# Attention plus SwiGLU on one Trainium2 core: group loads on 128 partitions, x by quadrants, and a DMA transpose of the normalised q

## The chip, the cores and the metric

The kernel runs on one core of a Trainium2 chip. Its time is the device time of one execution in microseconds. I quote medians of several executions. "Span" is the time from the first to the last instruction in a profile; it is about 2 us shorter than the timed value of the same execution (348.6 against 350.33 us before the change). A run is called slow when it lies over 1.5% above the fastest run of its kernel. In the views, PE is TensorE, PEld its loading of weights, DVE VectorE, ACT ScalarE, POOL GpSimd and SP the sync engine, and a q behind a name stands for that engine's sequencer, which issues its DMAs. PSUM is the memory that the matmuls of this kernel write to, in eight buffers that I call banks.

The kernel before was timed at 352.37 us when the prediction was made (median of 3 runs, 352.28 to 354.62).

## The reference, cut to what matters

```python
# q, k, v: [batch 8, heads 8, seq 576, head_dim 64], float32
q_s = exp(q - max(q, -1));  q_s = q_s / sum(q_s, -1)      # softmax over head_dim
k_s = exp(k - max(k, 2));   k_s = k_s / sum(k_s, 2)       # softmax over seq
kv  = einsum('bhsd,bhse->bhde', k_s, v)                   # 64 x 64 for each head
attn = einsum('bhsd,bhde->bhse', q_s, kv)
x   = attn.transpose(0, 2, 1, 3).reshape(4608, 512)       # tokens x (head, dim)
out = (silu(x @ w_gate) * (x @ w_val)) @ w_out            # d_ff 1536
```

The three large products are nearly all of the arithmetic. The attention needs q with the head dimension on the partitions (so q is transposed), and it needs x with its 512 features on the partitions, because x is the streamed operand of the gate and value products.

## The kernel before: the parts that matter

The kernel keeps x transposed in `xt` and works through one batch of attention ahead of the products. A batch has two groups of four heads. A group is loaded with heads on the two halves of the 128 partitions, each half by its own DMA:

```python
def load(b, G, what, src, second=None, after=None):
    t_ = ld.tile([128, 2, T * 64], FP32, tag=what, name=what)
    for g in range(2):                      # two DMAs, each to 64 partitions
        ap = bass.AP(tensor=src.tensor, offset=src[b, 4 * G + 2 * g].offset,
                     ap=[[T * 64, 64], [HSTR, 2], [1, T * 64]])
        ...
        d = eng.dma_start(out=t_[64 * g:64 * g + 64], in_=ap)
```

The attention of a group is a "head" (`att_exp` and `att_norm`: two exponentials on ScalarE, a cast of v, then a sum, a reciprocal and a multiplication on VectorE that give `qs`) and three steps:

```python
def att_t(b, G, eng):        # step 1: nine TensorE transposes of qs, copied out of PSUM
    for t0, t1 in BANKS:
        for t in range(t0, t1):
            nc.tensor.transpose(out=tp[...], in_=s["qs"][:, t, :], identity=ident)
        copy(eng, qt[:, :, t0:t1, :], tp[...])
def att_kv(b, G): ...        # step 2: k'v, 18 matmuls of 64 rows; its 129th column is the sum of k'
def att_bd(b, G): ...        #         k'v divided by that sum, into block-diagonal tiles bd
def att_x(b, G):             # step 3: x, full 128x128 matmuls with bd as weights
    for g in range(2):
        nc.tensor.matmul(out=xp[g], lhsT=s["bd"][:, g, :], rhs=qt[:, g, 0:512], ...)
        nc.tensor.matmul(out=tl[:, g, :], lhsT=s["bd"][:, g, :], rhs=qt[:, g, 512:S], ...)
    ...                      # three copies from PSUM to xt
```

`m_unit(c0, n, m)` is eight matmuls, four for gate and four for value, of one 128-wide slice of d_ff; ScalarE then applies silu (`sg`) and VectorE multiplies (`hr`). `o_unit(j)` is twelve matmuls of the output product. The schedule after batch 0 is written by hand:

```python
        ...                                   # batch 0: attention, then 12 m_units of 576 columns
        att_head(1, 0); o_unit(0); att_head(1, 1); load_batch(2); ...   # batch 1
        chunks = [(S, 448)] + [(c, 512) for c in range(1024, n_tok, 512)]
        for ci, (c0, n) in enumerate(chunks):         # chunk ci carries attention of batch ci + 2
            ...
            for m in range(MT):
                if m in (4, 8):
                    if att:
                        G = 0 if m == 4 else 1
                        att_head(b, G)
                        steps = att_steps(b, G)
                        if G == 1 and b + 1 < B:
                            load_batch(b + 1)
                    if ci > 0:
                        o_unit(...); o_unit(...)      # the first chunk has none
                m_unit(c0, n, m)
                if m % 4 > 0 and m > 4 and steps:
                    steps.pop(0)()
```

The first chunk is special. It has no `o_unit` in it, so TensorE has less work there between a head and the step that needs it.

The softmax here doesn't subtract the row's maximum and nothing guards it: scores larger than these inputs give would overflow.

Of the kernel before, what the change touches and what calls it, by code (L numbers as in the profile page):

```python
# [15 lines left out]
def kernel(  # L16
# [7 lines left out]
    moe_w_out: bass.AP,  # L24
    out: bass.AP,
):



# [4 lines left out]
    nc = tc.nc  # L34
# [24 lines left out]
    hr = const.tile([128, MT, RING], BF16, name="hr", tag="hr")  # L59
    ident = const.tile([128, 128], BF16, name="ident", tag="ident")  # L60
    vbs = [const.tile([128, T, 130], BF16, name=f"vb{i}", tag=f"vb{i}") for i in range(2)]
    bds = [const.tile([128, 2, 128], BF16, name=f"bd{i}", tag=f"bd{i}") for i in range(2)]

    dmas = {}
    raw = {}

    def load(b, G, what, src, second=None, after=None):
        t_ = ld.tile([128, 2, T * 64], FP32, tag=what, name=what)
        for g in range(2):
            ap = bass.AP(  # L70
                tensor=src.tensor,
                offset=src[b, 4 * G + 2 * g].offset,
                ap=[[T * 64, 64], [HSTR, 2], [1, T * 64]],
            )
            eng = second if g == 1 and second is not None else nc.sync
            d = eng.dma_start(out=t_[64 * g:64 * g + 64], in_=ap)  # L76
            if after is not None and g == 0:
                tc.add_manual_dep(d.ins, after.ins.name, SYNC, reason="order of loads")
        dmas[what, b, G] = d
        raw[what, b, G] = t_  # L80

    def load_batch(b, after=None):
        for G in range(NG):
            for what, src in (("q", q), ("k", k), ("v", v)):
                load(b, G, what, src, nc.scalar if (b, G, what) == (0, 0, "q") else None, after)
                after = None

    def w_slice(dst, src, c0, n):
# [23 lines left out]
    BANKS = ((0, 5), (5, 9))  # L112

    def att_exp(b, G, v_eng):
        s = st[b, G] = {"bd": bds[G], "vb": vbs[G]}
        for what in ("q", "k"):
            e = at.tile([128, T, 2, 64], BF16, tag="e" + what, name="e" + what)
            nc.scalar.activation(  # L118
                out=e, in_=raw[what, b, G].rearrange("p h (t d) -> p t h d", d=64), func=AF.Exp
            )  # L120
            s["e" + what] = e
        copy(
            v_eng,
            s["vb"][:, :, 0:128].rearrange("p t (h d) -> p t h d", d=64),
            raw["v", b, G].rearrange("p h (t d) -> p t h d", d=64),
        )
# [18 lines left out]
    def att_t(b, G, eng):  # L145
        s = st[b, G]
        qt = at.tile([128, 2, T, 64], BF16, tag="qt", name="qt")
        for t0, t1 in BANKS:
            tp = psp.tile([128, 1024], BF16, tag="ps", name="tp")
            for t in range(t0, t1):  # L150
                j = t - t0
                nc.tensor.transpose(  # L152
                    out=tp[:, j * 128:(j + 1) * 128], in_=s["qs"][:, t, :], identity=ident
                )
            copy(
                eng,
                qt[:, :, t0:t1, :],
                tp[:, 0:(t1 - t0) * 128].rearrange("p (t g c) -> p g t c", g=2, c=64),
            )
        s["qt"] = qt  # L160

    def att_kv(b, G):
        s = st[b, G]
# [9 lines left out]
                    stop=(t == T - 1),  # L173
                )

    def att_bd(b, G):
        s = st[b, G]
        for g in range(2):
            kv = s["kv"][g]
            kvr = at.tile([128, 1], FP32, tag=f"kvr{g}", name="kvr")  # L180
            nc.vector.reciprocal(out=kvr, in_=kv[:, 128:129])
            for h in range(2):
                r = slice(64 * h, 64 * h + 64)
                nc.vector.tensor_scalar_mul(s["bd"][r, g, r], kv[r, r], kvr[r, :])

    def att_x(b, G):
        s = st.pop((b, G))
        qt = s["qt"].rearrange("p g t c -> p g (t c)")
        xp = [f_tile("xp") for _ in range(2)]
        tl = f_tile("x_tail").rearrange("p (g c) -> p g c", g=8)  # L190
        for g in range(2):
            nc.tensor.matmul(  # L192
                out=xp[g], lhsT=s["bd"][:, g, :], rhs=qt[:, g, 0:512], start=True, stop=True
            )
            nc.tensor.matmul(  # L195
                out=tl[:, g, :], lhsT=s["bd"][:, g, :], rhs=qt[:, g, 512:S],
                start=True, stop=True,
            )
        c0 = b * S
        nc.scalar.copy(out=xt[:, 2 * G, c0:c0 + 512], in_=xp[0])  # L200
        nc.vector.tensor_copy(out=xt[:, 2 * G + 1, c0:c0 + 512], in_=xp[1])  # L201
        nc.scalar.copy(out=xt[:, 2 * G:2 * G + 2, c0 + 512:c0 + S], in_=tl[:, 0:2, :])


    def m_unit(c0, n, m):
        ms = slice(m * 128, (m + 1) * 128)
        parts = [(c0, n)] if n <= 512 else [(c0, n // 2), (c0 + n // 2, n // 2)]
        gu = []
        for w, nm in ((wg, "g_ps"), (wv, "u_ps")):
            ps = [f_tile(nm) for _ in parts]  # L210
            for kk in range(KT):
                for p_, (c, w_) in zip(ps, parts):
                    nc.tensor.matmul(  # L213
                        out=p_[:, 0:w_], lhsT=w[:, kk, ms], rhs=xt[:, kk, c:c + w_],
                        start=(kk == 0), stop=(kk == KT - 1),
                    )
            gu.append(ps)
        for g_ps, u_ps, (c, w_) in zip(gu[0], gu[1], parts):
            r = c % RING
            sg = ff.tile([128, 512], BF16, tag="sg", name="sg")  # L220
            nc.scalar.activation(out=sg[:, 0:w_], in_=g_ps[:, 0:w_], func=AF.Silu)  # L221
            nc.vector.tensor_mul(hr[:, m, r:r + w_], sg[:, 0:w_], u_ps[:, 0:w_])  # L222
# [38 lines left out]
    with tc.manual_schedule():  # L261
# [3 lines left out]
        nc.scalar.activation(out=warm, in_=warm, func=AF.Exp)  # L265
        for vb in vbs:
            nc.vector.memset(vb[:, :, 128:129], 1.0)
        for bd in bds:
            nc.vector.memset(bd, 0.0)

        w_dma = []
        for c0, n in ((0, 256), (256, 384), (640, 384), (1024, 512)):
# [11 lines left out]
        att_norm(0, 1, BANKS)  # L284
        att_t(0, 1, nc.scalar)
        att_kv(0, 1)
        att_bd(0, 0)
        att_x(0, 0)
        att_bd(0, 1)
        att_x(0, 1)  # L290

        load_batch(1, w_dma[-3])
# [8 lines left out]
        def att_steps(b, G):  # L301
            def kv_bd():
                att_kv(b, G)
                att_bd(b, G)
            return [lambda: att_t(b, G, nc.vector), kv_bd, lambda: att_x(b, G)]

        att_head(1, 0)
        o_unit(0)
# [14 lines left out]
        for ci, (c0, n) in enumerate(chunks):  # L323
# [1 line left out]
            first_o = 4 * ci  # L325
            att = b < B
            final = ci == len(chunks) - 1
            steps = []
            for m in range(MT):
                if m in (4, 8):  # L330
                    if att:
                        G = 0 if m == 4 else 1
                        att_head(b, G)
                        steps = att_steps(b, G)
                        if G == 1 and b + 1 < B:
                            load_batch(b + 1)
                    if ci > 0:
                        o_unit(first_o + (0 if m == 4 else 2))
                        if not (final and m == 8):
                            o_unit(first_o + (1 if m == 4 else 3))  # L340
                m_unit(c0, n, m)
                if m % 4 > 0 and m > 4 and steps:
                    steps.pop(0)()
        o_unit(first_o + 3)
        last = n_tok // 128 - 4
        for j in range(last, last + 3):
# [32 lines left out]
```

## Time and profile before

| stage of the trace before | us |
|---|---|
| start to the first gate matmul (attention of batch 0) | 25.29 |
| gate and value of batch 0 | 24.77 |
| batch 1: four output units and attention of batch 1 | 17.92 |
| first chunk (448 columns, attention of batch 2) | 27.96 |
| the rest: five chunks with attention (one of them measured: 35.01 us), two without, and the end | 252.61 |

The stages are cut at the first gate matmul, the first output matmul, the first gate matmul of 448 columns and the first of 512 columns.

The page of the kernel before shows, for each engine, busy time and instructions; then the busy tenths of TensorE and its granted clock in 40 slices of 8.7 us; then the shares of the chain that ended last:

```profile
PE 317.0 (91%) x1900; PEld 159.5 (46%) x1900; DVE 188.5 (54%) x354; ACT 152.6 (44%) x217; POOL 27.2 (8%) x31
PE   0269998998699999999999999999999999999994
PEclk9999999899999999999999999999999999999999
PE 80%; DVE 7%; DMA 7%; ACT 3%; issue 1%; SPq 1%; DVEq 0%; ACTq 0%
```

TensorE bounds the kernel after the first 100 us: its slices read 9. Before that they read 0, 2, 6, then 8, 8 and 6 in the middle. Those are the start, batch 1 and the first chunk.

The windows of the kernel before at the start give busy time (and instructions) of each engine, then the granted clock, the DMA share and GB/s:

```profile
core 0: us, PE busy (x) PEld busy (x) DVE busy (x) ACT busy (x) POOL busy (x), PEclk, DMA share, GB/s
4.00:8.00 4.00, 0.00 (x0) 0.00 (x0) 0.70 (x1) 1.16 (x1) 0.00 (x0) 1.00 1.05 221
8.00:12.00 4.00, 1.21 (x9) 0.89 (x10) 3.26 (x6) 1.72 (x2) 0.34 (x1) 1.00 1.04 227
12.00:16.00 4.00, 1.16 (x18) 0.89 (x17) 0.77 (x1) 1.75 (x2) 4.00 (x6) 1.00 1.05 229
```

TensorE and ScalarE are mostly idle, and the DMA share reads full (1.04 to 1.05) at 221 to 229 GB/s. (VectorE is busy for 3.26 us of the second window, and GpSimd fills the third with issuing the loads of the weights.) The start is bound by loads.

In the timeline of the kernel before, the two transposes of the first chunk are the only waits of TensorE over 2 us after batch 0's attention (columns: start, duration, engine, line, what, and in brackets the idle time before it and what ended it):

```profile
80.12 0.68 PE L152 MATMUL tp<-ident,qs 128*128 128x128 bf16 x9 [2.41 <-DVE qs L138]
91.18 0.68 PE L152 MATMUL tp<-ident,qs 128*128 128x128 bf16 x9 [3.10 <-DVE qs L138]
```

The timeline of TensorE in a full chunk of the kernel before shows what the three steps cost. Matmuls overlap (the gate group at 147.40 lasts 1.03 us, and the next starts 0.86 us after it), so the cost of a group is the distance to the next start, not its duration:

```profile
130.89 0.94 PE L213 MATMUL g_ps<-xt,wg 128*128 128x512 bf16 x3
132.01 0.38 PE L213 MATMUL g_ps<-xt,wg 128*128 128x512 bf16 x1 [0.18 <-DVE xt L201]
132.22 1.02 PE L213 MATMUL u_ps<-xt,wv 128*128 128x512 bf16 x4
...
146.90 0.67 PE L152 MATMUL tp<-ident,qs 128*128 128x128 bf16 x9
147.40 1.03 PE L213 MATMUL g_ps<-xt,wg 128*128 128x512 bf16 x4
...
151.59 0.38 PE L192 MATMUL xp<-qt,bd_78 128*128 128x512 bf16 x1
```

Nine transposes take 0.50 us (146.90 to 147.40). From the start of x at 151.59 to the next group at 152.08 it is 0.49 us. k'v takes 0.63 us (149.22 to 149.85, not shown). The first three lines are the first gate group behind the last x of a batch: its fourth matmul waits for a copy to `xt`, and the group takes 1.33 us (130.89 to 132.22) where a group of four takes 0.86 elsewhere (147.40 to 148.26, not shown).

### The profile page before, as it was taken

How to read it: one execution, taken by the hardware profiler on the slowest of the kernel's cores; microseconds unless marked ns; L12 is line 12 of the kernel's file. 1: busy time of each engine (PE TensorE's matmuls, PEld its weight loads, DVE VectorE, ACT ScalarE, POOL GpSimd, SP SyncE). 2: the span in 40 equal slices, each digit the busy share in tenths (PEclk: the TensorE clock that was granted, in tenths of full speed). 3: DMA queues.
4: the chain of work that ended last, by engine and by line, in shares of the span. 5: the costliest groups of instructions: out<-in, count | busy, mean ns of one | idle time of the engine just before them, and what ended most of it. 6: DMA issues, size and time to landing. Idle time of an engine off the chain costs nothing.

```text
span 348.6 us, 5035 instructions
## 1 busy us (share of the span) xinstructions
PE 317.0 (91%) x1900; PEld 159.5 (46%) x1900; DVE 188.5 (54%) x354; ACT 152.6 (44%) x217; POOL 27.2 (8%) x31
## 2 busy tenths in 40 slices
PE   0269998998699999999999999999999999999994
PEld 0237773444344454444444444444445444444443
DVE  2553439647746674667466746674667433333331
ACT  3454353376655734563456345634663311322200
POOL 0620012111100011002100110011000000000000
PEclk9999999899999999999999999999999999999999
DMA  7999998999602990299029902990202021102123
GB/s 168 228 200 206 226 230 198 230 255 224 131 0 47 231 248 5 60 224 241 5 59 222 244 5 55 212 229 34 51 11 61 1 63 29 31 2 60 30 62 91
DMA packets 25577, 42.81 MB, mean 123 GB/s; under 512 B 2896, under 2 KB 8784, under 8 KB 25552
## 3 DMA queue, kind: packets, MB, share of 16 engines
q1 hardware_dynamic: 19440, 37.33, 46.6%
q0 software_dynamic: 5808, 4.72, 8.6%
q10 hardware_dynamic: 304, 0.43, 0.5%
q8 instruction: 15, 0.25, 0.3%
q14 instruction: 10, 0.08, 0.1%
HBM read 37.75 MB, written 9.44 MB: 135 GB/s over the span
## 4 chain that ended last, share of the span: by engine, by line
PE 80%; DVE 7%; DMA 7%; ACT 3%; issue 1%; SPq 1%; DVEq 0%; ACTq 0%
PE u_ps L213 25%; PE g_ps L213 25%; PE o_ps L238 24%; DMA v<-in_v_dram 5%; PE kv L168 2%; PE tp L152 2%; DMA k<-in_k_dram 2%; DVE xt L201 1%; DVE hr L222 1%; PE xp L192 1%; DVE qs L138 1%; DVE rs L132 1%; ACT L118 1%; ACT eq L118 1%; SPq L76 1%
## 5 line engine op out<-in xcount | busy, mean ns | idle before, releaser
L221 ACT ACTIVATE sg<-g_ps 128x512 bf16<-128x512 f32 (+2 forms) x120 | 65.0, 554 | 146.0 <-PE g_ps L213 145.9
L222 DVE TENSOR_TENSOR hr<-sg,u_ps 128x512 bf16<-128x512 bf16 (+2 forms) x120 | 74.8, 633 | 91.2 <-PE u_ps L213 89.5
L213 PE MATMUL g_ps<-xt,wg 128*128 128x512 bf16 (+2 forms) x480 | 114.1, 361 | 1.2 <-DVE xt L201 0.9
L213 PE MATMUL u_ps<-xt,wv 128*128 128x512 bf16 (+2 forms) x480 | 111.3, 359 | 0.0
L238 PE MATMUL o_ps<-wo,hr 128*128 128x512 bf16 x420 | 94.1, 380 | 0.0
L213 PEld LDWEIGHTS <-wv 128*128 128x128 bf16 x480 | 47.1, 98 | 49.0 <-issue 3.1
L213 PEld LDWEIGHTS <-wg 128*128 128x128 bf16 x480 | 45.2, 99 | 43.0 <-issue 2.0
L238 PEld LDWEIGHTS <-hr 128*128 128x128 bf16 x420 | 40.7, 98 | 49.0 <-issue 0.8
L132 DVE TENSOR_REDUCE rs<-eq 128x18 f32<-128x1152 bf16 x16 | 21.6, 1353 | 32.9 <-ACT eq L118 32.9
L243 DVE COPY o_sb<-o_ps 128x512 f32<-128x512 f32 x35 | 23.2, 685 | 22.1 <-PE o_ps L238 22.1
L152 PE MATMUL tp<-ident,qs 128*128 128x128 bf16 x144 | 12.2, 236 | 19.5 <-DVE qs L138 19.4
L138 DVE TENSOR_TENSOR qs<-eq,rr 128x1152 bf16<-128x1152 bf16 (+2 forms) x18 | 21.9, 1224 | 0.5
L108 POOL CAST vb_76<-v 128x1152 bf16<-128x1152 f32 x7 | 9.2, 1310 | 150.3 <-DMA v<-in_v_dram 89.1
L152 PEld LDWEIGHTS <-qs 128*128 128x128 bf16 x144 | 9.9, 105 | 24.0 <-DVE qs L138 21.2
L118 ACT ACTIVATE eq<-q 128x1152 bf16<-128x1152 f32 x16 | 18.6, 1163 | 4.8 <-DMA q<-in_q_dram 4.6
L118 ACT ACTIVATE ek<-k 128x1152 bf16<-128x1152 f32 x16 | 18.4, 1150 | 4.4 <-DMA k<-in_k_dram 4.4
L221 ACT ACT_TABLE_LOAD x14 | 18.0, 1283 | 0.2
L200 ACT CAST xt<-xp 128x512 bf16<-128x512 f32 x16 | 9.4, 586 | 17.6 <-PE xp L192 9.4
L118 ACT ACT_TABLE_LOAD x13 | 16.7, 1283 | 0.2
L168 PEld LDWEIGHTS <-ek 64*128 64x128 bf16 x288 | 9.7, 102 | 8.5 <-ACT sg L221 5.0
L201 DVE CAST xt<-xp 128x512 bf16<-128x512 f32 x16 | 10.9, 684 | 3.4 <-PE x_tail L195 3.4
L108 POOL CAST vb_77<-v 128x1152 bf16<-128x1152 f32 x7 | 9.0, 1289 | 44.9 <-DMA v<-in_v_dram 24.9
(38 smaller groups left out, 102.0 us busy)
## 6 DMA issues: line engine op xcount, KB each, us to landing
k<-in_k_dram SPq DMA_DIRECT2D x32, 288.0 KB, 8.8
v<-in_v_dram SPq DMA_DIRECT2D x32, 288.0 KB, 9.7
out_dram<-o_sb SPq DMA_DIRECT2D x70, 128.0 KB, 2.4
q<-in_q_dram SPq DMA_DIRECT2D x31, 288.0 KB, 7.7
wo<-in_moe_w_out_dram POOLq DMA_DIRECT2D x3, 512.0 KB, 18.7
wg<-in_moe_w_gate_dram POOLq DMA_DIRECT2D x2, 384.0 KB, 11.0
wv<-in_moe_w_val_dram POOLq DMA_DIRECT2D x2, 384.0 KB, 12.2
wg<-in_moe_w_gate_dram POOLq DMA_DIRECT2D x1, 512.0 KB, 16.8
```

The lines of the kernel that those rows point to most:

```text
L108: eng.tensor_copy(out=out, in_=in_)
L118: nc.scalar.activation(out=e, in_=raw[what, b, G].rearrange("p h (t d) -> p t h d", d=64), func=AF.Exp)
L132: nc.vector.reduce_sum(out=rs, in_=eq2, axis=mybir.AxisListType.X)
L138: nc.vector.tensor_mul(qs[:, t0:t1, :].rearrange("p t (h d) -> p (t h) d", d=64), eq2[:, 2 * t0:2 * t1, :], rr[:, 2 * t0:2 * t1].to_broadc ...
L152: nc.tensor.transpose(out=tp[:, j * 128:(j + 1) * 128], in_=s["qs"][:, t, :], identity=ident)
L168: nc.tensor.matmul(out=kv[g][:, 0:129], lhsT=s["ek"][r, t, :, :].rearrange("p h d -> p (h d)"), rhs=s["vb"][r, t, 0:129], start=(t == 0), ...
L201: nc.vector.tensor_copy(out=xt[:, 2 * G + 1, c0:c0 + 512], in_=xp[1])
L213: nc.tensor.matmul(out=p_[:, 0:w_], lhsT=w[:, kk, ms], rhs=xt[:, kk, c:c + w_], start=(kk == 0), stop=(kk == KT - 1),)
L221: nc.scalar.activation(out=sg[:, 0:w_], in_=g_ps[:, 0:w_], func=AF.Silu)
L222: nc.vector.tensor_mul(hr[:, m, r:r + w_], sg[:, 0:w_], u_ps[:, 0:w_])
L238: nc.tensor.matmul(out=o_ps, lhsT=hr[:, m, r0:r0 + 128], rhs=wo[:, m, :], start=(m == 0), stop=(m == MT - 1),)
L243: nc.vector.tensor_copy(out=o_sb, in_=o_ps)
```

## The change

The intent has three parts.

1. A group tensor is loaded by one DMA to all 128 partitions instead of two to 64 each. The two partition halves now hold heads 4G+g and 4G+2+g instead of 4G+2g and 4G+2g+1.
2. x is computed by 64x64 quadrants, so that a head can be read from one half of the partitions and written to the other. The block-diagonal tiles go. In batch 0, the scaling of k'v is shared by VectorE and ScalarE.
3. From batch 2 on, a DMA transposes `qs` from SBUF to SBUF, and TensorE no longer does it. The heads and steps are moved one unit earlier (in the first chunk, the heads three).

```diff
-        for g in range(2):
-            ap = bass.AP(..., offset=src[b, 4 * G + 2 * g].offset,
-                         ap=[[T * 64, 64], [HSTR, 2], [1, T * 64]])
-            d = eng.dma_start(out=t_[64 * g:64 * g + 64], in_=ap)
+        ap = bass.AP(..., offset=src[b, 4 * G].offset,
+                     ap=[[T * 64, 128], [2 * HSTR, 2], [1, T * 64]])
+        d = nc.sync.dma_start(out=t_, in_=ap)
 ...
+    def att_t_dma(b, G):
+        qt = at.tile([128, T, 2, 64], BF16, tag="qtd", name="qtd")
+        nc.sync.dma_start_transpose(out=qt.rearrange("p t g c -> p t (g c)"),
+                                    in_=s["qs"].rearrange("p t c -> p (t c)"))
 ...
-                nc.vector.tensor_scalar_mul(s["bd"][r, g, r], kv[r, r], kvr[r, :])
+                if split and g == 1:
+                    nc.scalar.mul(kn[r, g, :], kv[r, r], kvr[r, :])
+                else:
+                    nc.vector.tensor_scalar_mul(kn[r, g, :], kv[r, r], kvr[r, :])
 ...
+        for t0, t1 in BANKS:
+            for g in range(2):
+                for h in range(2):
+                    r = slice(64 * h, 64 * h + 64)
+                    nc.tensor.matmul(out=xp[h][64 * g:64 * g + 64, 0:n]...,
+                                     lhsT=s["kn"][r, g, :], rhs=s["qt"][g][r, t0:t1, :], ...)
 ...
-                if m in (4, 8):                       # heads of the two groups
+            heads = {1: 0, 5: 1} if ci == 0 else {3: 0, 7: 1}
+                if att and m in heads:
+                    att_head(b, G)
+                    att_t_dma(b, G)
+                    for i, f in enumerate(att_steps(b, G)):
+                        steps[4 + 4 * G + i] = f      # nothing, kv and bd, x
```

Two smaller edits are not shown. The first q load, of which ScalarE's queue had issued one half, now goes through the sync queue whole. And an `m_unit` of batch 0 is cut into 320 and 256 columns instead of 288 and 288.

More of the change, by code (lines that the diff above doesn't have):

```diff
@@ L61, with load @@
     vbs = [const.tile([128, T, 130], BF16, name=f"vb{i}", tag=f"vb{i}") for i in range(2)]
-    bds = [const.tile([128, 2, 128], BF16, name=f"bd{i}", tag=f"bd{i}") for i in range(2)]
     dmas = {}
     raw = {}
-    def load(b, G, what, src, second=None, after=None):
+    def load(b, G, what, src, after):
         t_ = ld.tile([128, 2, T * 64], FP32, tag=what, name=what)
-        for g in range(2):
-            ap = bass.AP(
-                tensor=src.tensor,
-                offset=src[b, 4 * G + 2 * g].offset,
-                ap=[[T * 64, 64], [HSTR, 2], [1, T * 64]],
-            )
-            eng = second if g == 1 and second is not None else nc.sync
-            d = eng.dma_start(out=t_[64 * g:64 * g + 64], in_=ap)
-            if after is not None and g == 0:
-                tc.add_manual_dep(d.ins, after.ins.name, SYNC, reason="order of loads")
+        ap = bass.AP(
+            tensor=src.tensor,
+            offset=src[b, 4 * G].offset,
+            ap=[[T * 64, 128], [2 * HSTR, 2], [1, T * 64]],
+        )
+        d = nc.sync.dma_start(out=t_, in_=ap)
+        if after is not None:
+            tc.add_manual_dep(d.ins, after.ins.name, SYNC, reason="order of loads")
         dmas[what, b, G] = d
@@ L84, in load_batch @@
             for what, src in (("q", q), ("k", k), ("v", v)):
-                load(b, G, what, src, nc.scalar if (b, G, what) == (0, 0, "q") else None, after)
+                load(b, G, what, src, after)
                 after = None
@@ L114, in att_exp @@
     def att_exp(b, G, v_eng):
-        s = st[b, G] = {"bd": bds[G], "vb": vbs[G]}
+        s = st[b, G] = {"vb": vbs[G]}
         for what in ("q", "k"):
@@ L159, in att_t @@
             )
-        s["qt"] = qt
+        s["qt"] = [qt[:, g, :, :] for g in range(2)]
+    def att_t_dma(b, G):
+        s = st[b, G]
+        qt = at.tile([128, T, 2, 64], BF16, tag="qtd", name="qtd")
+        nc.sync.dma_start_transpose(
+            out=qt.rearrange("p t g c -> p t (g c)"),
+            in_=s["qs"].rearrange("p t c -> p (t c)"),
+        )
+        s["qt"] = [qt[:, :, g, :] for g in range(2)]
     def att_kv(b, G):
@@ L174, in att_kv, with att_bd @@
                 )
-    def att_bd(b, G):
+    def att_bd(b, G, split):
         s = st[b, G]
+        kn = s["kn"] = at.tile([128, 2, 64], BF16, tag="kn", name="kn")
         for g in range(2):
@@ L183, in att_bd @@
                 r = slice(64 * h, 64 * h + 64)
-                nc.vector.tensor_scalar_mul(s["bd"][r, g, r], kv[r, r], kvr[r, :])
+                if split and g == 1:
+                    nc.scalar.mul(kn[r, g, :], kv[r, r], kvr[r, :])
+                else:
+                    nc.vector.tensor_scalar_mul(kn[r, g, :], kv[r, r], kvr[r, :])
     def att_x(b, G):
         s = st.pop((b, G))
-        qt = s["qt"].rearrange("p g t c -> p g (t c)")
-        xp = [f_tile("xp") for _ in range(2)]
-        tl = f_tile("x_tail").rearrange("p (g c) -> p g c", g=8)
-        for g in range(2):
-            nc.tensor.matmul(
-                out=xp[g], lhsT=s["bd"][:, g, :], rhs=qt[:, g, 0:512], start=True, stop=True
-            )
-            nc.tensor.matmul(
-                out=tl[:, g, :], lhsT=s["bd"][:, g, :], rhs=qt[:, g, 512:S],
-                start=True, stop=True,
-            )
-        c0 = b * S
-        nc.scalar.copy(out=xt[:, 2 * G, c0:c0 + 512], in_=xp[0])
-        nc.vector.tensor_copy(out=xt[:, 2 * G + 1, c0:c0 + 512], in_=xp[1])
-        nc.scalar.copy(out=xt[:, 2 * G:2 * G + 2, c0 + 512:c0 + S], in_=tl[:, 0:2, :])
+        for t0, t1 in BANKS:
+            n = 64 * (t1 - t0)
+            xp = [f_tile("xp") for _ in range(2)]
+            for g in range(2):
+                for h in range(2):
+                    r = slice(64 * h, 64 * h + 64)
+                    nc.tensor.matmul(
+                        out=xp[h][64 * g:64 * g + 64, 0:n].rearrange("p (t c) -> p t c", c=64),
+                        lhsT=s["kn"][r, g, :],
+                        rhs=s["qt"][g][r, t0:t1, :],
+                        start=True, stop=True,
+                    )
+            c0 = b * S + 64 * t0
+            nc.scalar.copy(out=xt[:, 2 * G, c0:c0 + n], in_=xp[0][:, 0:n])
+            nc.vector.tensor_copy(out=xt[:, 2 * G + 1, c0:c0 + n], in_=xp[1][:, 0:n])
     def m_unit(c0, n, m):
         ms = slice(m * 128, (m + 1) * 128)
-        parts = [(c0, n)] if n <= 512 else [(c0, n // 2), (c0 + n // 2, n // 2)]
+        parts = [(c0, n)] if n <= 512 else [(c0, 320), (c0 + 320, n - 320)]
         gu = []
@@ L267 @@
             nc.vector.memset(vb[:, :, 128:129], 1.0)
-        for bd in bds:
-            nc.vector.memset(bd, 0.0)
         w_dma = []
@@ L286 @@
         att_kv(0, 1)
-        att_bd(0, 0)
+        att_bd(0, 0, True)
         att_x(0, 0)
-        att_bd(0, 1)
+        att_bd(0, 1, True)
         att_x(0, 1)
@@ L303, in kv_bd @@
                 att_kv(b, G)
-                att_bd(b, G)
-            return [lambda: att_t(b, G, nc.vector), kv_bd, lambda: att_x(b, G)]
+                att_bd(b, G, False)
+            if b == 1:
+                return [lambda: att_t(b, G, nc.vector), kv_bd, lambda: att_x(b, G)]
+            return [lambda: None, kv_bd, lambda: att_x(b, G)]
         att_head(1, 0)
@@ L327 @@
             final = ci == len(chunks) - 1
-            steps = []
+            heads = {1: 0, 5: 1} if ci == 0 else {3: 0, 7: 1}
+            steps = {}
             for m in range(MT):
-                if m in (4, 8):
-                    if att:
-                        G = 0 if m == 4 else 1
-                        att_head(b, G)
-                        steps = att_steps(b, G)
-                        if G == 1 and b + 1 < B:
-                            load_batch(b + 1)
-                    if ci > 0:
-                        o_unit(first_o + (0 if m == 4 else 2))
-                        if not (final and m == 8):
-                            o_unit(first_o + (1 if m == 4 else 3))
+                if att and m in heads:
+                    G = heads[m]
+                    att_head(b, G)
+                    att_t_dma(b, G)
+                    for i, f in enumerate(att_steps(b, G)):
+                        steps[4 + 4 * G + i] = f
+                    if G == 1 and b + 1 < B:
+                        load_batch(b + 1)
+                if ci > 0 and m in (3, 7):
+                    o_unit(first_o + (0 if m == 3 else 2))
+                    if not (final and m == 7):
+                        o_unit(first_o + (1 if m == 3 else 3))
                 m_unit(c0, n, m)
-                if m % 4 > 0 and m > 4 and steps:
-                    steps.pop(0)()
+                if m in steps:
+                    steps[m]()
         o_unit(first_o + 3)
```

## The prediction

> **What bounds the kernel now.** TensorE: busy 317.0 us of a 348.6 us span (the page's busy times); the chain that ended last is 80% TensorE. Exceptions, from timeline and windows:
>
> - 0 to 25.3 us: batch 0 is loaded and transformed; the chain names the k and v loads for 16.6 us. A 590 KB pair lands every 2.57 us, 221 to 229 GB/s (4 us windows). Last v is used at 19.15, first gate matmul at 25.3.
> - 50 to 68 us (batch 1): VectorE delays x.
> - 68 to 97 us (first chunk): TensorE stands 2.4 and 3.1 us before the transposes, waiting for normalised q (waits by line).
> - Then five almost gapless chunks of 35.0 us.
>
> **Costs in such a chunk.** Gate/up 96 x 0.216 = 20.7; out 48 x 0.216 = 10.4; the rest is attention: per group 9 transposes 0.51, kv 0.73, x 0.49 us (timeline), and about 0.25 at the chunk's end, where the first gate matmul waits for the last xt copy.
>
> **What the change does.**
>
> 1. 128-partition loads. [...] With k'v scaled on two engines, the first gate matmul moves to about 19.5: **-5.5 us**. Batch 1 is loaded well before use, but VectorE bounds that stage: **-0.5**.
> 2. Crossbar transpose from batch 2. Removes 12 x 0.51 us of TensorE and 0.82 us VectorE copies (off the path). In the first chunk 5.5 us of idle goes, but there the second head now delays VectorE before the first group's k'v scaling: a new wait of 2 to 3.5 us. Net **-4.5** for that chunk.
>    [...] From a head to its x lie two out units (5.2), four gate/up units (6.9) and kv (0.7); q is ready 5.5 us in. Slack about 7 us, so hidden. No run yet shows it.
> 3. x in quadrants. kv already runs 64-row matmuls side by side (18 of 129 columns in 0.63 us), so I expect 0.3 to 0.4 us instead of 0.49: about **-0.15** per group. Moving the steps one unit earlier removes most of the 0.25 at chunk ends.
>    Five chunks: 5 x (1.0 + 0.3 + 0.25) = **-8**.
>
> **Sum:** about -18.5: **334 us**, 8 in 10 from 326 to 342. Faster by over 2%: 0.90; within 2%: 0.07; slower: 0.03.
>
> **What would show it.** First gate matmul at 18.5 to 21; [...]chunks of about 33.4 us; no idle at transposes in the first chunk; transposes landing under 6 us; x of a group under 0.45 us.
>
> **What would make it wrong.** A transpose that takes over 7 us, or holds the sync queue so that loads and stores behind it are late: x would stall in every chunk. Quadrant matmuls that do not overlap (0.96 us per group). Weights that arrive after the earlier gate matmuls.

-5.5 - 0.5 - 4.5 - 8 = -18.5, which takes 352.37 to about 334. For the "hidden" of the transpose the slack of about 7 us is worked out from the trace, and the time to landing was not shown by any trace. The 0.96 us for quadrants that do not overlap is an estimate from the trace: eight matmuls, 2304 columns in all, at the full chunk's 0.216 us for 512. "Crossbar transpose" is only the author's name for the transpose by DMA of part 3.

## The result, and the profile after

The changed kernel took 337.65 us (median of 4 runs, 336.84 to 338.56). The kernel before took 353.5 us in the same rounds (4 runs, 352.28 to 354.86). The ratio is 0.955, with a 95% interval of 0.950 to 0.961. Every ratio in this document is the mean time of one kernel's fast runs over the mean of the other's of the same rounds, so it is not quite the ratio of the medians that I quote. The prediction of 334 us was 3.65 us low, and the time lies in the range of 326 to 342.

The two profiled executions took 350.33 and 338.56 us. Their spans differ by 12.2 us, less than the medians do. The kernel before scatters with its granted clock: in its later rounds, runs at a mean clock of 0.995 took 350 to 353 us, and one at 0.982 took 354.1. The profiled execution was one of the quick ones. So I compare the stages of traces with each other and not with the medians.

| stage, us | before | after | difference | predicted |
|---|---|---|---|---|
| start to first gate matmul | 25.29 | 19.86 | -5.43 | -5.5 |
| gate and value of batch 0 | 24.77 | 25.63 | +0.86 | 0 |
| batch 1 | 17.92 | 18.11 | +0.19 | -0.5 |
| first chunk | 27.96 | 28.71 | **+0.75** | **-4.5** |
| the rest | 252.61 | 244.03 | -8.58 | -8 |

The page after:

```profile
PE 312.7 (93%) x1828; PEld 152.7 (45%) x1856; DVE 180.4 (54%) x340; ACT 152.5 (45%) x221; POOL 25.1 (7%) x31
PE   0689997995999999999999999999999999999995
PEclk9999999896999999999999999999999999999999
PE 83%; DVE 5%; DMA 4%; ACT 4%; issue 1%; SPq 0%
```

The first two slices of TensorE are fuller. The slices of batch 1 and the first chunk (7, 9, 9, 5) are not better than before, and the clock has dropped to 6 tenths in one of them. (The 8 in batch 1 stands in both pages: in both traces the clock records also show half the clock for 3.41 us there.)

The windows of the start, after:

```profile
4.00:8.00 4.00, 0.00 (x0) 0.00 (x0) 2.22 (x3) 2.33 (x2) 0.00 (x0) 1.00 1.02 378
8.00:12.00 4.00, 2.37 (x27) 1.78 (x27) 2.56 (x5) 2.81 (x3) 3.23 (x5) 1.00 1.09 366
12.00:16.00 4.00, 2.24 (x30) 1.69 (x30) 3.04 (x8) 3.28 (x6) 3.86 (x6) 1.00 1.34 185
```

With the same DMA share of about 1, the loads now move 366 to 378 GB/s. The last window is already the weights, which the kernel converts from float32 to bfloat16 while it loads them.

The timeline of a full chunk, after:

```profile
108.57 1.04 PE L225 MATMUL g_ps<-xt,wg 128*128 128x512 bf16 x4
109.45 1.03 PE L225 MATMUL u_ps<-xt,wv 128*128 128x512 bf16 x4
110.41 0.44 PE L206 MATMUL xp<-qtd,kn 64*64 64x320 bf16 x8
```

The transposes are gone and nothing waits in their place. The next group starts at 110.78, 0.37 us after the start of x. But x itself starts 0.10 us late: four matmuls of 512 columns take 0.86 us from start to start here, and from 109.45 to 110.41 it is 0.96. So x costs 0.47 us, about what it cost before. A full chunk went from 35.01 us to 33.51 us (first output matmul to first output matmul: 138.26 to 173.27 before, 131.00 to 164.50 after).

The first chunk of the changed kernel on TensorE:

```profile
74.81 0.92 PE L225 MATMUL u_ps<-xt,wv 128*128 128x448 bf16 x4
79.41 1.84 PE L206 MATMUL xp<-qtd,kn 64*64 64x320 bf16 x8 [3.68 <-DVE kn L196]
81.18 1.68 PE L225 MATMUL g_ps<-xt,wg 128*128 128x448 bf16 x4
82.65 1.70 PE L225 MATMUL u_ps<-xt,wv 128*128 128x448 bf16 x4
84.14 1.65 PE L225 MATMUL g_ps<-xt,wg 128*128 128x448 bf16 x4
85.63 0.92 PE L225 MATMUL u_ps<-xt,wv 128*128 128x448 bf16 x4
```

And VectorE in that stretch:

```profile
75.39 1.35 DVE L131 TENSOR_REDUCE rs<-eq 128x18 f32<-128x1152 bf16 x1 [1.55 <-ACT eq L117]
77.08 1.36 DVE L137 TENSOR_TENSOR qs<-eq,rr 128x1152 bf16<-128x1152 bf16 x1
78.35 0.61 DVE L234 TENSOR_TENSOR hr<-sg,u_ps 128x448 bf16<-128x448 bf16 x1
79.08 0.60 DVE L196 TENSOR_SCALAR kn<-kv,kvr 64x64 bf16<-64x64 f32 x2
```

Three things cost time here. TensorE stands 3.68 us before x of batch 2's first group, until VectorE has scaled k'v. VectorE had first to do the head of the second group (75.39 to 78.4), which stands ahead of it in its queue. Then x itself stretches over 1.77 us (79.41 to 81.18) instead of 0.37. And after it three groups of four matmuls start 1.47 to 1.49 us apart instead of 0.76, so they run at half rate. In the trace's clock records the granted clock is at half from 78.79 to 85.62.

There is a smaller finding in batch 0. The first gate matmuls come earlier, but the clock is still low:

```profile
19.86 2.10 PE L225 MATMUL g_ps<-xt,wg 128*128 128x320 bf16 x8
21.76 2.12 PE L225 MATMUL u_ps<-xt,wv 128*128 128x320 bf16 x8
```

They start 1.90 us apart; at full rate it is 0.98 (below). The clock column of the windows reads 1.00 here. The clock records of this trace begin with the rise at 24.18, and before the first record the column says nothing. The distance of the starts is the reading to trust. This stage scatters: in the traces of the other runs with the same code here it took 24.97 to 25.85 us, so the +0.86 of the table is one draw of +0.2 to +1.1.

### The profile page after: what moved, and what is told of

It is laid out like the page before. It is cut to its first block, busy times and chain, and to the rows that moved or that the text cites. A ratio compares the mean times of both kernels' runs of the same rounds, so it can differ in the third digit from the quotient of the medians.

```text
span 336.3 us, 4853 instructions
## 1 busy us (share of the span) xinstructions
PE 312.7 (93%) x1828; PEld 152.7 (45%) x1856; DVE 180.4 (54%) x340; ACT 152.5 (45%) x221; POOL 25.1 (7%) x31
## 4 chain that ended last, share of the span: by engine, by line
PE 83%; DVE 5%; DMA 4%; ACT 4%; issue 1%; SPq 0%
PE g_ps L225 27%; PE u_ps L225 27%; PE o_ps L250 24%; PE kv L176 2%; PE xp L206 2%; DMA q<-in_q_dram 2%; DMA out_dram<-o_sb 2%; DVE rs L131 2%; ACT eq L117 1%; ACT L117 1%; DVE qs L137 1%; ACT sg L233 1%; PE o_ps L264 1%; DVE kn L196 1%; DVE o_sb L255 1%
## 5 line engine op out<-in xcount | busy, mean ns | idle before, releaser
L225 PE MATMUL g_ps<-xt,wg 128*128 128x512 bf16 (+2 forms) x466 | 112.5, 365 | 0.8 <-ACT xt L213 0.2
L225 PEld LDWEIGHTS <-wg 128*128 128x128 bf16 x480 | 46.1, 100 | 47.4 <-issue 4.2
L107 POOL CAST vb_76<-v 128x1152 bf16<-128x1152 f32 x7 | 8.0, 1149 | 170.5 <-DMA v<-in_v_dram 142.4
L213 ACT CAST xt<-xp 128x320 bf16<-128x320 f32 (+1 forms) x32 | 11.4, 401 | 20.3 <-PE xp L206 20.3
L196 DVE TENSOR_SCALAR kn<-kv,kvr 64x64 bf16<-64x64 f32 x60 | 17.0, 283 | 2.0
L214 DVE CAST xt<-xp 128x320 bf16<-128x320 f32 (+1 forms) x32 | 13.0, 449 | 2.8 <-PE xp L206 2.8
L151 PE MATMUL tp<-ident,qs 128*128 128x128 bf16 x36 | 3.8, 264 | 11.3 <-DVE qs L137 11.2
L206 PEld LDWEIGHTS <-kn 64*64 64x64 bf16 x128 | 3.7, 109 | 15.4 <-DVE kn L196 13.9
```

The costliest lines, as they stand in the source:

```text
L196: nc.vector.tensor_scalar_mul(kn[r, g, :], kv[r, r], kvr[r, :])
L213: nc.scalar.copy(out=xt[:, 2 * G, c0:c0 + n], in_=xp[0][:, 0:n])
L214: nc.vector.tensor_copy(out=xt[:, 2 * G + 1, c0:c0 + n], in_=xp[1][:, 0:n])
L225: nc.tensor.matmul(out=p_[:, 0:w_], lhsT=w[:, kk, ms], rhs=xt[:, kk, c:c + w_], start=(kk == 0), stop=(kk == KT - 1),)
```

## The experiments

My theory after the result had these parts: the start gains by the 128-partition loads alone; the transposes by DMA gain 0.5 us each; the quadrants gain nothing; and the first chunk's gain is eaten by a wait of the schedule's making, and by a clock that the wait lets fall. The rival for the first chunk was that the loads of batch 3, which are issued from 79.84 on, disturb TensorE or VectorE. The rival for the start was that the split scaling of k'v has a share in it.

The first four runs share runs of the kernel before (median 350.8 us, 7 runs). The next four share those of a second call on the same chip (median 351.59, 11 runs). best and best2 ran on two other chips, each with its own runs of the kernel before (350.94 and 351.92).

### kv_first: k'v of the first group before the head of the second, in the first chunk

```diff
                 if att and m in heads:
                     G = heads[m]
+                    if ci == 0 and G == 1:
+                        steps.pop(5)()        # kv and bd of group 0
                     att_head(b, G)
```

> The changed kernel, but in the first chunk the k'v product and its scaling for batch 2, group 0 stand before the second head (exp, reduce, multiply) instead of after it. In the changed kernel's profile TensorE stands 3.68 us there (75.7 to 79.4 us) waiting for kn, and its matmuls then run at about half rate until 85.6 us. Theory A (VectorE's order makes the wait[...]): the idle shrinks to under 1.5 us, no halved matmuls follow, the first chunk falls from 28.7 to 21 to 22.5 us, and the kernel gains 6 to 8 us over the changed one. Rival B (the halved matmuls come from the loads of batch 3, which start at 79.8 us): only the idle goes, 2 to 3.7 us, and the halved matmuls stay. Rival C (x really waits for the crossbar transpose): no gain at all, 0 plus or minus 1 us.

Measured: 334.71 us, ratio 0.954 (0.951 to 0.958). The first chunk took 25.34 us, where 28.71 was the value after. That is half of the gain that I expected: the kernel is 2.9 us below late_loads (further down), which is in effect the changed kernel. TensorE in the timeline:

```profile
75.00 0.44 PE L206 MATMUL xp<-qtd,kn 64*64 64x320 bf16 x8
77.54 1.65 PE L225 MATMUL g_ps<-xt,wg 128*128 128x448 bf16 x4 [2.10 <-ACT sg L233]
```

x no longer waits, and it takes 0.44 us. So the order of the head and k'v made the 3.68 us. But a second wait shows: the next gate group waits 2.10 us for `sg`. ScalarE does the second head's two exponentials (1.16 and 1.15 us) with a table load of 1.28 us before and one after them, and the gate group starts at 77.54, right behind the first silu after them (76.95, 0.54 us), which reads a PSUM bank. In the changed kernel that wait was covered by the longer one. The clock fell to half here too, from 77.58 to 80.99. By its size, 2 to 3.7 us with the slow matmuls left, this is what rival B forecast; what speaks against B is the order in time, since the first load of batch 3 goes out at 79.09, after the fall. Rival C, a wait for the transpose, is refuted by x at 75.00. Here the clock fell behind a gap of 2.10 us, where it was 3.68 in the changed kernel.

### warm_fill: dummy matmuls in the gap

```diff
                 m_unit(c0, n, m)
+                if ci == 0 and m == 6:
+                    fill = f_tile("fill")
+                    for _ in range(16):
+                        nc.tensor.matmul(out=fill, lhsT=ident, rhs=xt[:, 0, 0:512], ...)
```

> The changed kernel, with 16 dummy matmuls of 512 columns into a spare PSUM bank in the 3.68 us gap before the x of batch 2, group 0; nothing else moves, so x still cannot start before about 79.4 us. Theory A (idle lets the clock fall): x and the matmuls after it run at full rate (0.19 us per 448 columns), the first chunk falls from 28.7 to about 24.2 us, the kernel gains 4 to 5 us. Rival B (the batch 3 loads slow the matmuls): matmuls at 80 to 85.6 us still take about 0.37 us each and the kernel gains under 1 us.

Measured: 336.11 us, ratio 0.957 (0.953 to 0.960); first chunk 26.29 us.

```profile
75.48 3.62 PE L359 MATMUL fill<-xt,ident 128*128 128x512 bf16 x16
79.32 0.64 PE L206 MATMUL xp<-qtd,kn 64*64 64x320 bf16 x2 [0.23 <-DVE kn L196]
...
80.84 0.93 PE L225 MATMUL g_ps<-xt,wg 128*128 128x448 bf16 x4
```

The dummies do nothing but keep TensorE at work. x still waits until 79.32, and it still stretches, to 80.84, because its operands come one by one. But the matmuls after it run at full rate, and this trace's granted clock reads 1.00 from 64 to 92 us. So the clock's share of the loss is 28.71 - 26.29 = 2.42 us (2.28 against the 28.57 of late_loads). I had expected 4 to 5 for it. The whole kernel is only 1.5 us below late_loads; in the traces its batch 0 stage was 0.5 us longer. The loads of batch 3 begin at 79.76 in this run and the matmuls that run beside them are quick. That goes against the rival.

### late_loads: the loads of batch 3 later (the edit did not do what it was for)

```diff
-                    if G == 1 and b + 1 < B:
+                    if G == 1 and b + 1 < B and ci > 0:
                         load_batch(b + 1)
+                if ci == 0 and m == 9:
+                    load_batch(b + 1)
```

> The changed kernel, with the loads of batch 3 issued four gate/up units later in the first chunk (before unit 9), so that none runs beside the half-rate matmuls at 80 to 85.6 us. Theory A (clock after idle): the matmuls there are still at half rate and the time does not change (within 1 us). Rival B (contention with loads at 260 to 390 GB/s): the matmuls there run at full rate and the kernel gains about 4.5 us.

Measured: 337.61 us, ratio 0.962 (0.958 to 0.965); first chunk 28.57 us. This decides nothing, because the loads did not move. The timeline of the sync engine's queue:

```profile
77.79 1.29 SPq L164 DMA_TRANSPOSE qtd<-qs  x1
79.17 0.54 SPq L75 DMA_DIRECT2D q<-in_q_dram  x1
```

The first load goes out at 79.17, right behind the transpose. The sync queue holds nothing else in the first chunk, so it runs ahead of TensorE: the load that the program places before unit 9 went out 6.4 us before that unit's first matmul (85.58). Moving the loads to a later place in the program did not make them later. The run is in effect a repeat of the changed kernel. The rival is refuted by the other runs: in warm_fill the loads run and the rate is full, in kv_first the half rate begins at 77.5, before its first load at 79.09, in the changed kernel the clock falls at 78.79 and the first load goes out at 79.84, and in the changed kernel's batch 0 stage from 36 to 40 us the DMA moves 401 GB/s beside 35 matmuls in 4 us, which is full rate (at half rate, from 20 to 24 us, it was 18).

### loads64: two 64-partition loads again, all else as changed

```diff
+        for g in range(2):
+            ap = bass.AP(..., offset=src[b, 4 * G + g].offset,
+                         ap=[[T * 64, 64], [2 * HSTR, 2], [1, T * 64]])
+            d = nc.sync.dma_start(out=t_[64 * g:64 * g + 64], in_=ap)
```

> The changed kernel with every group tensor again loaded by two 64-partition DMAs, with the same heads on the same partitions; all else stays. Theory ([...]batch 0's loads bound the start): DMA windows in the first 16 us fall from about 370 to about 225 GB/s, the first gate matmul moves from 19.9 to 24.5 to 25.5 us, and the kernel loses 5 to 6 us against the changed one; nothing later changes, since loads have slack there. Rival (the earlier start came from scaling k'v on two engines and from the x quadrants): it loses under 2 us.

Measured: 343.65 us, ratio 0.980 (0.975 to 0.985), which does not settle whether this kernel is faster by over 2%. Start to the first gate matmul 25.36 us, as before the change; all other stages within 0.6 us of the changed kernel's. A window of the start:

```profile
4.00:8.00 4.00, 0.00 (x0) 0.00 (x0) 0.90 (x1) 1.16 (x1) 0.00 (x0) 1.00 1.01 233
```

The rate is back at 233 GB/s (230 and 227 in the next two windows) with the same bytes and the same tile. So the gain at the start is the loads', and the split scaling of k'v adds nothing to it that shows: from the use of the last v to the first gate matmul it was 6.14 us before (19.15 to 25.29), 6.41 here (18.95 to 25.36) and 6.90 after the change (12.96 to 19.86). By the windows, loads of 64 partitions moved 221 to 233 GB/s and loads of 128 partitions 366 to 378; why, no run here shows.

### after_again: the changed kernel, unchanged

No edit; it gives the value to compare with.

> The changed kernel unaltered, as the measure for the others of this call: within 0.6% of its first ratio to the kernel before, 0.955.

Measured: 337.52 us, ratio 0.959 (0.956 to 0.962), first chunk 28.74 us, with the first groups of gate matmuls again 1.90 us apart (18.99 and 20.89). The result and its stages repeat. Here the difference of the medians is 14.1 us.

### pe_transpose: TensorE transposes throughout, all else as changed

```diff
-            if b == 1:
+            if True:
                 return [lambda: att_t(b, G, nc.vector), kv_bd, lambda: att_x(b, G)]
 ...
-                    att_t_dma(b, G)
```

> The changed kernel with q transposed on TensorE for all batches, at units 4 and 8 (the step that the changed kernel leaves empty); loads, quadrants and the places of the heads stay. Theory (what the crossbar saves is 9 transposes of 57 ns per group on a full TensorE, and the DMA is hidden): each full chunk grows from 33.5 to 34.5 us and the kernel loses 5 to 6.5 us against the changed one. Rival (the gain of the chunks came from moving heads and steps one unit earlier, and the crossbar gives back what it saves by holding the sync queue for 1.3 us and the loads behind it): it loses under 2 us.

Measured: 343.3 us, ratio 0.977 (0.974 to 0.980), 5.8 us above after_again. A full chunk takes 34.51 us instead of 33.51.

```profile
104.57 0.67 PE L151 MATMUL tp<-ident,qs 128*128 128x128 bf16 x9
```

The next group starts at 105.07, so the nine transposes of a group cost 0.50 us. In the traces the ten groups of the five full chunks make 5.0 us. The first chunk is no longer than after_again's (28.47 against 28.74), because TensorE waits there in both, and the rest of the 5.8 lies in the last microseconds (17.66 us from the last long run of output matmuls to the end, against 16.95), where the code is the same; I count it as scatter. So in the full chunks the DMA transpose gains what TensorE no longer does, and nothing of it is given back there.

The DMA view of the changed kernel (what, engine, count, median us from issue to landing):

```profile
qtd<-qs SPq DMA_TRANSPOSE x12, 3.3
```

The slowest of the twelve took 5.0 us, and in the full chunks no x waited for one. The issue itself holds the sync queue for 1.3 us.

### x_full: block-diagonal 128x128 matmuls for x (wrong on purpose)

```diff
-                for h in range(2):
-                    r = slice(64 * h, 64 * h + 64)
-                    nc.tensor.matmul(out=xp[h][64 * g:64 * g + 64, 0:n]..., lhsT=s["kn"][r, g, :], ...)
+                nc.tensor.matmul(out=xp[g][:, 0:n]..., lhsT=s["kn"][:, g, :],      # kn = bd
+                                 rhs=s["qt"][g][:, t0:t1, :], ...)
```

With the new loads the heads lie in other places, so this kernel puts them in the wrong rows of x. Its result is wrong (relative error 1.23); only its time is of use.

> The changed kernel with x by block-diagonal 128x128 matmuls again (two per bank instead of four 64x64 quadrants). With this change's load the heads then come out on the wrong channels: WRONG RESULT ON PURPOSE, only the time counts. From the traces a group's x takes 0.47 us of TensorE's time with its 0.10 us entry gap in quadrants and 0.50 us in full tiles. Theory (the four quadrants run side by side, but streaming was cheap already and the entry gap takes most of it back; what quadrants do is let a 128-partition load feed x without moving partitions): within 0.6 us of the changed kernel. My prediction's size (0.15 us per group, 16 groups): it loses about 2.4 us.

Measured: 336.8 us, ratio 0.958 (0.955 to 0.960), 0.7 us below after_again. A full chunk takes 33.53 us against 33.51.

```profile
122.48 0.65 PE L206 MATMUL xp<-qtd,bd 128*128 128x320 bf16 x4
```

The next group starts at 122.97, 0.49 us later. The quadrants take 0.37 us but begin 0.10 us late, so they gain almost nothing. No run here takes the 0.10 us at the entry apart. What the quadrants are for is the placing of heads: they let part 1 of the change be done without moving data between partitions.

### warm_start: dummy matmuls before batch 0's gate product

```diff
         att_kv(0, 0)
+        spin(6)                      # six matmuls of ident with 512 columns of vb
         att_norm(0, 1, BANKS)
 ...
         att_x(0, 0)
+        spin(4)
```

> The changed kernel with 6 and 4 dummy matmuls of 512 columns in TensorE's gaps before batch 0's second transposes and before its second x, so that TensorE is nearly always busy from about 11 us on. In the changed kernel the first gate/up matmuls (19.9 to 23.7 us) take 1.7 us per 8 instead of 0.98. Theory (the clock is still low because TensorE was mostly idle before): the first gate matmul starts at about 19.5 us, the groups take 0.98 us from the first or second on, the kernel gains 1 to 2.5 us. Rival (those matmuls are slow because weights arrive or are read at the same time): no gain, within 0.5 us.

Measured: 335.47 us, ratio 0.954 (0.951 to 0.956), 2.05 us below after_again. Batch 0's gate and value stage took 23.53 us instead of 25.63.

```profile
19.18 1.15 PE L231 MATMUL g_ps<-xt,wg 128*128 128x320 bf16 x8
20.17 1.14 PE L231 MATMUL u_ps<-xt,wv 128*128 128x320 bf16 x8
```

The starts are 0.98 to 0.99 us apart from the first group on. So the 0.86 us that this stage lost after the change is the clock: in the kernel before, 24.77 - 23.53 = 1.24 us went the same way, and 2.10 in the changed one. The clock records agree: from the first gate matmul to the rise of the clock it was 2.57 us before (25.29 to 27.86) and 4.32 us after (19.86 to 24.18).

### best: both causes in one kernel, first try

The dummies of warm_start, the loads of batch 2 moved forward, the exponentials of batch 2 moved into the batch 1 stage (there ScalarE of the changed kernel idles for 6.43 and 5.47 us and has no table load between 45.33 and 64.32), and this first chunk:

```diff
+                if ci == 0:
+                    if m == 0:    att_norm(2, 0, whole); att_t_dma(2, 0); load_batch(3)
+                    elif m == 2:  att_kv(2, 0); att_bd(2, 0, False)
+                    elif m == 4:  att_norm(2, 1, whole); att_t_dma(2, 1)
+                    elif m == 5:  att_x(2, 0)
+                    elif m == 7:  att_kv(2, 1); att_bd(2, 1, False)
+                    elif m == 9:  att_x(2, 1)
```

In the batch 1 stage, the heads, k'v and x of batch 1 are reordered too: k'v of both groups is scaled on both engines before the second head's normalisation, ScalarE takes part in the copies out of the transposes, and three dummies stand before the last x.

> The changed kernel with what the runs so far point to, all in the first 95 us; full chunks and tail stay. (1) The dummy matmuls of the warm start. (2) Batch 2's loads are issued earlier and its exps run on ScalarE in the batch 1 stage, where ScalarE is idle and still holds the exp table, so the first chunk has no head that blocks ScalarE for 4.9 us. (3) In the batch 1 stage both k'v products and their scaling, shared by two engines, come before the second normalisation. (4) In the first chunk k'v and its scaling come two units before x. Theory (these waits are order on VectorE and ScalarE plus the clock that falls after them): start to first gate matmul unchanged at 19 to 19.5 us, the batch 1 stage from 18.1 to about 15 us, the first chunk from 28.7 to 20.7 to 22 us, no halved clock after 60 us; 324 to 328 us, against 337.5 for the changed kernel. Rival (the first chunk is bound by something else, such as PSUM banks or the transposes' landing): 331 us or more.

Measured: 332.3 us, ratio 0.945 (0.941 to 0.950; the kernel before 350.94, 11 runs). Batch 1 fell to 15.96 us, but the first chunk only to 26.90. The timelines of TensorE and of the sync queue, and the spread of the landings, show why:

```profile
70.78 4.74 SPq L164 DMA_TRANSPOSE qtd<-qs  x1
79.81 0.69 PE L206 MATMUL xp<-qtd,kn 64*64 64x320 bf16 x8 [4.36 <-DMA qtd<-qs]
DMA to landing us min/median/max: 3.2/3.3/9.0
```

By the number this is my rival's result, and the cause is one that it named, the landing of a transpose. I had put the six loads of batch 3 (3.5 MB) into the queue ahead of the second group's transpose. The issue of that transpose held the queue for 4.74 us instead of 1.3, and it landed after 9.0 us. x waited 4.36 us for it, and the clock fell again (the two groups behind x took 1.47 and 1.33 us to the next start instead of 0.76). A transpose that takes over 7 us is a danger that the prediction names; the changed kernel had avoided it by issuing transposes ahead of loads.

### best2: the loads of batch 3 behind that transpose

```diff
                     if m == 0:
                         att_norm(2, 0, whole); att_t_dma(2, 0)
-                        load_batch(3)
 ...
                     elif m == 4:
                         att_norm(2, 1, whole); att_t_dma(2, 1)
+                        load_batch(3)
```

> The last kernel with one line moved: the loads of batch 3 are issued after the second crossbar transpose of the first chunk instead of before it. In the last run that transpose stood behind 3.5 MB of loads in the same queue, held the sync sequencer 4.74 us and landed 9.0 us after its issue instead of 3.3, and the x of batch 2, group 1 waited 4.36 us for it; the clock then fell for 3.4 us. Theory (queueing behind the load burst made the transpose late): all 12 transposes land in 3.2 to 5 us, that wait and the fall of the clock are gone, the first chunk falls from 26.9 to 20.7 to 21.5 us, and the kernel takes 325 to 328 us. Rival (the second transpose is late for another reason, such as the multiply before it): the wait stays and the time is 331 us or more.

Measured: 325.27 us (324.85 to 325.63, 6 runs), ratio 0.925 (0.922 to 0.928; the kernel before 351.92, 11 runs). The result is correct. The first chunk took 20.95 us. The landings, x of the second group, and the clock of the page:

```profile
DMA to landing us min/median/max: 3.2/3.2/3.4
75.71 0.44 PE L206 MATMUL xp<-qtd,kn 64*64 64x320 bf16 x8
PEclk9999999999999999999999999999999999999999
```

No group waits for a head, all twelve transposes land in 3.2 to 3.4 us, and the clock does not fall after the start (9 in all 40 slices; 1.000 in the mean). Against the changed kernel's trace (span 336.3, here 323.2): start -0.72, batch 0 -2.10, batch 1 -2.61, first chunk -7.76, the rest +0.02. This version beats both kernels.

## Why the prediction was right or wrong

The time was in the range and the direction was right. The parts are not all right, and that the total came out only 3.65 us off is partly luck: in the traces the change gains 12.2 us where 18.5 was forecast. The 334 was counted from the median of 352.37, while the profiled execution of the kernel before, one of the quick ones, took 350.33.

- **Start: right.** Predicted -5.5, the traces show -5.43. The last v of batch 0 was used at 12.96 instead of 19.15. loads64 puts the stage back to 25.36, so it is the 128-partition loads that make the gain.
- **Weights ahead of the gate product: right, with a price.** The prediction names late weights as a danger. They did arrive in time: no wait for them stands before the groups at 19.86 and 21.76. What was not in the sum is the clock: the earlier gate matmuls ran at half rate for longer, +0.86 us in this trace and +0.2 to +1.1 in others. warm_start shows the cause.
- **Batch 1: wrong and small.** Predicted -0.5, measured +0.19. Before its first x TensorE still waits for VectorE's scaling of k'v (1.57 us before, 1.27 after), and the clock falls to half behind that wait in both traces, for 3.41 us (61.99 to 65.41 before, 58.31 to 61.72 after). best2, which reorders this stage, takes 2.61 us less; no run takes the stage apart.
- **First chunk: this is the term that failed.** The prediction put it as "Net **-4.5** for that chunk", made of 5.5 us of idle that goes, "a new wait of 2 to 3.5 us", and smaller gains that it doesn't spell out for this chunk (by its other terms two transposes, two x and a chunk's end, about 1.5 us). The measured change is +0.75. The old waits did go. The new wait was named and placed correctly, and it was 3.68 us, just over the upper end. But two costs that follow from it were left out. x came in pieces, as VectorE delivered its operands one by one: 1.77 us to the next group here, 1.52 us in warm_fill at full rate, 0.37 us where nothing is late. And the clock fell to half after the wait: 2.42 us by warm_fill. With x at its warm 1.52 us, the sum of the losses is 3.68 + (1.52 - 0.37) + 2.42 = 7.25 us. The gains were 2.41 + 3.10 us of old waits and 2 x 0.50 of transposes, 6.51 us; the other smaller gains did not come in this chunk. The balance is a loss of 0.74, and 0.75 was measured; the terms come from several traces, so a match to 0.01 is chance. kv_first and best2 show that the order of the steps is the root: once k'v is scaled before the second head the wait goes, and once the exponentials are also done ahead the chunk falls to 20.95.
- **The transposes by DMA: right.** Predicted under 6 us to land and hidden; measured 3.2 to 3.3 as a rule, 5.0 at worst, and hidden in the full chunks. pe_transpose confirms 0.5 us each.
- **x by quadrants: the term was wrong, with no harm.** Predicted -0.15 us a group; x_full shows about zero, because the entry costs 0.10 us.
- **Steps one unit earlier: mis-sized in our favour.** A full chunk gained 1.50 us. Two transposes are 1.0 of it and the quadrants about 0, so about 0.5 is left for the moved steps, where I had written 0.25. pe_transpose, which has the moved steps and TensorE's transposes, shows the same 0.5: 34.51 us instead of 35.01. In the timeline of before, the gate group behind the last x of a batch waits for a copy to xt (132.01, 167.02, 202.03) and takes 1.33 us instead of 0.86, which is 0.47; after the change no such wait is left in the full chunks. No run moves the steps alone.
- **The rest: right.** -8 predicted, -8.58 in the traces, of which 5 x 1.50 = 7.5 are the five chunks. Of what remains, 0.67 us lie in the last microseconds, where the code did not change.

One thing is still open: what exactly makes the clock fall. In these traces it stood after a gap of 3.10 us and one of 2.41 us (kernel before, first chunk), and it fell after a gap of 2.10 us (kv_first) and, in batch 1 of the changed kernel, at 58.31 after one of 1.27 us (before the x at 56.19). I tried the busy time in stretches of 3.41 us, as long as the fall in batch 1: one with 1.95 us of work (54.90 to 58.31, changed kernel) was followed by a fall and another with 1.54 us (89.30 to 92.72, kernel before) was not. Neither the gap alone nor that busy time tells the cases apart.

## What to carry to other kernels

When a step is taken off an engine, write down what its consumer will wait for next and in which order that engine's queue will deliver it; a wait of 3.7 us on TensorE here cost about 7.3 us, because it also spread the next step out and let the clock fall. Put a transfer that something waits for ahead of the prefetches in its queue, never behind them: here it landed after 3.2 us instead of 9.0. And read a low clock from the distance between the starts of equal matmuls (1.90 us for a group here, where it is 0.98 at full rate), and keep TensorE at work with a few dummies ahead of a long dense stage, which was worth 2 us here.
